# Windowed attention ahead of two feed-forward layers: the softmax division moved from the probabilities to the output

## The chip, the cores and the metric

One of the eight cores of a Trainium2 chip runs the whole program. Its engines are TensorE (PE for its matmuls, PEld for its weight loads), VectorE (DVE), ScalarE (ACT), GpSimd (POOL) and SyncE (SP, which here only issues DMAs). Each works through its own list of instructions in order and waits on semaphores for the others. The metric is device time in microseconds of one execution; lower is better.

## The reference

Sixteen heads (2 batches of 8) of 768 positions and 64 columns attend to four sink positions and to the last 128 positions. The result, 1536 tokens by 512, goes through two feed-forward layers of 512 by 2048 by 512, each with its own activation.

```python
scores = scale * np.matmul(q, k.transpose(0, 1, 3, 2))
keep = is_sink | in_window
scores = np.where(keep, scores, -1000000000.0)
a = np.exp(scores - np.max(scores, axis=-1, keepdims=True))
a = a / (np.sum(a, axis=-1, keepdims=True) + 1e-09)
x = np.matmul(a, v)                       # then (tokens, heads * head_dim)
h = x @ w_in                              # first layer
g = np.where(h >= 1, h, np.where(h <= -1, 0.0, (h + 1) ** 2 / 4))
x = g @ w_out
h = x @ w2_in                             # second layer
g = np.where(h > 0.0, h, np.exp(np.minimum(h, 0.0)) - 1.0)
out = g @ w2_out
```

## The kernel before

**Attention.** The queries are cut into six segments (three for each batch) of two blocks of 128 rows, and the heads into four pairs, which gives 24 jobs (a segment and a pair). A job runs in five steps. `st_T` turns q and k by PE transposes (L444) and copies them to SBUF (L446); POOL writes the four sink keys behind each block of keys (L458, L463). `st_S`, once for each of the two query blocks, multiplies (L488) and has DVE apply the mask and take the maximum (L492, tile `nb`) and ACT the exponential with its row sum (L494, tile `sm`). With the second block come the reciprocals `r` of the sums (L501, L502), the four sink columns of both blocks, normalised, into `psn` (L505), and the normalisation of all of P: on DVE by head (L514), or on POOL for both heads at once (L509) for the jobs 8 to 15 (`POOLED`). `st_X` turns P by transposes (L536) and copies it (ACT, L538). `st_V` multiplies it by v (L561), and DVE copies the pair's output, with features on partitions and queries along the columns, to `xb` (L564).

After the fourth pair of a segment `st_sink` adds what the sink positions give: it turns `psn` for all heads (L573), splits the result into a rounded part and a remainder (`pst`, L575 to L577), multiplies it by the sinks' values `vs` (L585), adds that to `xb` (L588), and splits the sum into `xh` and `xl` (ACT L590, POOL L591), the input of the feed-forward layers. All of the layers' products are made of such pairs, three products for one.

**Feed-forward layers.** An item is a block of 512 tokens (three) and 128 of the 2048 hidden columns (16), for each of the two layers: 96 items. An item has 12 products for `h` (L172), the activation `g` and its split into `gh` and `gl` (L179 to L189), and 12 products into four sums `y` (L211), which follow two items later. Its weights are split anew into `wh` (ACT, L160) and `wl` (POOL, L161). The weights come from memory as 64-bit numbers, in units of 128 columns or rows: ACT, then DVE turn a unit into float32 (L140, L141 and L144, L145, L147), 32 units for each layer, the first layer's within its first 13 items.

**What sets the order.** The first two segments (jobs 0 to 7) run ahead of the first item. From then on every item calls `between` four times, and each call runs one step of the attention, until the six segments are done. From this program a scheduler makes the lists of the five engines, merging steps by its own estimate of their times; the lists are then fixed. Pools set how far work can run ahead: four P tiles, two PSUM banks for the attention once the items have begun (`bank`), one `xb`.

**The store.** In the last items the output sums are copied to one of two tiles of the pool `mt` (L274) and written out.

## Time and profile before

| what | value |
|---|---|
| median of 3 runs | 692.01 us (691.42 to 694.39) |
| the profiled execution, its own time | 691.88 us |
| its span, first to last instruction | 689.7 us |
| busy in the span: PE, DVE, ACT, POOL | 660.4, 406.0, 459.9, 315.3 us |
| mean granted clock of TensorE | 0.983 of 2.4 GHz |
| PE in h and y (L172, L211), instructions | 1152 and 1128 of 3112 |

The busy time of an engine is the union of its instructions' durations in the trace. Matmuls overlap in the pipeline, so that PE is shown as busy also where it starts instructions at less than its rate; what it starts, and what it waits for, is read from the order of time and from the list of waits. An idle time is put down to the engine whose semaphore came last before the instruction began. "issue" is time in which an engine waited for nothing that the profile shows. Shares of the whole span average over stages with different limits, so the rows below are by stage.

### The profile page before, as it was taken

To read this page: it belongs to the slowest core of one execution; us is meant where nothing else is said; L and a number is where in the kernel's file an instruction comes from. 1 tells how busy PE (TensorE), PEld (TensorE's weight loads), DVE (VectorE), ACT (ScalarE), POOL (GpSimd) and SP (SyncE) were. 2 spreads that over 40 slices of the span, in tenths; PEclk is the share of its full clock that TensorE was granted. 3 is DMA by queue.
4 is the path that set the end of the run, shared out by engine and by line. 5 is a ranking of instruction groups with operands and counts; after the bars stand their busy time and mean duration, and the time that the engine had idled before them with its cause. 6 is when DMAs were issued, how large, how long until landed. Compare 5 with 4: busy or idle time off the path is not lost.

```text
span 689.7 us, 9414 instructions
## 1 busy us (share of the span) xinstructions
PE 660.4 (96%) x3112; PEld 506.3 (73%) x3112; DVE 406.0 (59%) x839; ACT 459.9 (67%) x944; POOL 315.3 (46%) x278
## 2 busy tenths in 40 slices
PE   5998987889999999999999999999999999999996
PEld 3566665666767777788878888888888888888884
DVE  5788999899665565322788878777532222322221
ACT  5799887787766766555768877777655555555552
POOL 2324464474523433444445655555544444444431
PEclk9699999899999999999999999999999999999999
DMA  6465564366121000000143323232010000100001
GB/s 168 104 179 155 160 183 139 114 207 180 32 54 39 12 13 13 0 1 1 61 153 95 119 92 92 93 100 83 0 62 2 0 1 0 60 3 0 1 0 67
DMA packets 71018, 48.96 MB, mean 71 GB/s; under 512 B 48944, under 2 KB 65328, under 8 KB 70960
## 3 DMA queue, kind: packets, MB, share of 16 engines
q1 hardware_dynamic: 70672, 48.27, 24.2%
q8 instruction: 26, 0.43, 0.3%
q14 instruction: 32, 0.26, 0.1%
q10 hardware_dynamic: 288, 0.00, 0.0%
HBM read 45.11 MB, written 3.15 MB: 70 GB/s over the span
## 4 chain that ended last, share of the span: by engine, by line
PE 77%; DVE 14%; issue 4%; ACT 3%; SPq 1%; POOL 1%; DMA 0%; POOLq 0%; DVEq 0%; ACTq 0%
PE h L172 33%; PE y L211 32%; PE S L488 4%; DVE ca L145 3%; DVE F L147 3%; PE ops L561 3%; PE tps L536 3%; DVE ca L144 2%; DVE P L492 1%; DVE g L181 1%; DVE gl L189 1%; SPq L387 1%; PE kps L444 1%; ACT P L494 1%; PE qps L444 1%
## 5 line engine op out<-in xcount | busy, mean ns | idle before, releaser
L161 POOL TENSOR_TENSOR wl<-F,wh 128x512 fp32r<-128x512 f32 x192 | 262.8, 1372 | 296.4 <-ACT wh L160 261.4
L160 ACT CAST wh<-F 128x512 fp32r<-128x512 f32 x192 | 117.6, 617 | 99.1 <-PE h L172 88.8
L172 PE MATMUL h<-xh,wh 128*128 128x512 f32 x384 | 155.2, 405 | 2.4 <-DVE g L181 2.4
L172 PE MATMUL h<-xl,wh 128*128 128x512 f32 x384 | 152.0, 396 | 0.5 <-POOL xl L591 0.5
L172 PE MATMUL h<-xh,wl 128*128 128x512 f32 x384 | 151.7, 395 | 0.0
L188 ACT CAST gh<-g 128x512 fp32r<-128x512 f32 x96 | 59.6, 621 | 66.0 <-DVE g L185 36.1
L189 DVE TENSOR_TENSOR gl<-g,gh 128x512 fp32r<-128x512 f32 x96 | 73.0, 761 | 51.2 <-ACT gh L188 50.8
L185 DVE SCALAR_TENSOR_TENSOR g<-g,h 128x512 f32<-128x512 f32 x48 | 33.0, 687 | 115.5 <-ACT g L184 115.4
L172 PEld LDWEIGHTS h<-xh,wh 128*128 128x128 f32 x384 | 71.9, 187 | 22.4 <-DVE g L181 3.2
L147 DVE CUSTOM_DVE_ANT_0 F<-ca,F 128x1024 uint16<-128x1024 uint16 x64 | 81.6, 1275 | 5.7 <-DVE ca L145 1.8
L172 PEld LDWEIGHTS h<-xh,wl 128*128 128x128 f32 x384 | 71.9, 187 | 17.7
L172 PEld LDWEIGHTS h<-xl,wh 128*128 128x128 f32 x384 | 72.0, 188 | 16.5 <-POOL xl L591 1.1
L211 PE MATMUL y<-gh,wh 128*128 128x512 f32 x192 | 79.7, 415 | 0.0
L211 PE MATMUL y<-gl,wh 128*128 128x512 f32 x192 | 76.4, 398 | 0.0
L211 PE MATMUL y<-gh,wl 128*128 128x512 f32 x192 | 75.9, 395 | 0.0
L211 PE MATMUL y<-wl,gh 128*128 128x512 f32 x184 | 72.2, 392 | 0.0
L211 PE MATMUL y<-wh,gh 128*128 128x512 f32 x184 | 71.8, 390 | 0.0
L211 PE MATMUL y<-wh,gl 128*128 128x512 f32 x184 | 71.6, 389 | 0.0
L494 ACT ACTIVATE P<-P,nb 128x260 f32<-128x260 f32 (+1 forms) x96 | 46.7, 488 | 19.3 <-DVE nb L492 18.7
L181 DVE SCALAR_TENSOR_TENSOR g<-h,g 128x512 f32<-128x512 f32 x48 | 32.9, 685 | 44.2 <-ACT g L180 44.2
L145 DVE SCALAR_TENSOR_TENSOR ca<-st,ca 128x512 int32<-128x512 int32 x64 | 52.9, 826 | 1.5
L140 ACT ACTIVATE ca<-st 128x512 f32<-128x512 f32 x64 | 43.0, 672 | 5.2 <-DVE F L147 4.3
(103 smaller groups left out, 920.0 us busy)
## 6 DMA issues: line engine op xcount, KB each, us to landing
st<-in_moe_w_in_dram SPq DMA_DIRECT2D x32, 512.0 KB, 3.9
st<-in_moe_w_out_dram SPq DMA_DIRECT2D x32, 512.0 KB, 3.6
qn<-in_q_dram SPq DMA_DIRECT2D x48, 64.0 KB, 2.1
kn<-in_k_dram SPq DMA_DIRECT2D x32, 96.0 KB, 2.3
vn<-in_v_dram SPq DMA_DIRECT2D x32, 96.0 KB, 2.2
out_dram<-o SPq DMA_DIRECT2D x12, 256.0 KB, 2.2
kn<-in_k_dram SPq DMA_DIRECT2D x16, 64.0 KB, 2.9
vn<-in_v_dram SPq DMA_DIRECT2D x16, 64.0 KB, 2.1
```

The source lines that it names most:

```text
L140: nc.scalar.activation(a, w1.bitcast(F32), AF.Copy, scale=2.0 ** -112)
L145: nc.vector.scalar_tensor_tensor(out=ai, in0=w1, scalar=-0x80000000, in1=ai, op0=ALU.bitwise_and, op1=ALU.bitwise_or)
L147: nc.vector.tensor_tensor(out=r, in0=ai, in1=r, op=ALU.add)
L160: nc.scalar.copy(hi, src)
L161: nc.gpsimd.tensor_tensor(out=lo, in0=src, in1=f32(hi), op=ALU.subtract)
L172: nc.tensor.matmul(h, lhsT=w[:, k * 128:(k + 1) * 128], rhs=x[:, k, c0:c0 + n], start=(k == 0 and p == 0), stop=(k == self.KD - 1 and p == 2))
L181: nc.vector.scalar_tensor_tensor(out=g, in0=h, scalar=1.0, in1=g, op0=ALU.max, op1=ALU.min)
L185: nc.vector.scalar_tensor_tensor(out=g, in0=g, scalar=-1.0, in1=h, op0=ALU.add, op1=ALU.max)
L188: ac = nc.scalar.copy(gh, g)
L189: dv = nc.vector.tensor_tensor(out=gl, in0=g, in1=f32(gh), op=ALU.subtract)
L211: nc.tensor.matmul(self.y[c], lhsT=a, rhs=b, start=(first and p == 0), stop=(last and p == 2))
L494: ac = nc.scalar.activation(o, o, AF.Exp, bias=nb[:, n, h:h + 1], scale=-1.0, accum_out=sm[:, n, h:h + 1])
```

## The change

P stays as the exponential leaves it. `st_S` loses L501 to L514; in place of L505 POOL copies the four sink columns of each head, one instruction of eight columns for each job and block (48 in all), to one tile `psn` of a segment, and the row sums of all eight heads of a segment go to one tile `sm`. `st_sink` begins with four DVE instructions on 16 columns: the sums get 1e-9, the reciprocals, their rounded part and the remainder of the rounding, the last two behind the sinks in `psn`. The transposes then turn 48 columns instead of 32, ACT makes one more copy (16 partitions), and `pst` has 112 rows instead of 96. A constant `one` of 112 by 512, built once by POOL, has ones in the rows of the reciprocals: its product with `pst` (L595 in the new numbering) gives each reciprocal in all 64 rows of its head, `rps`, in a second PSUM bank beside `xps`. DVE adds `xps` to `xb` as before and then multiplies by `rps`. `vs` gets 16 rows of zeros. The store uses the tiles `g` and `ca` in place of `g` and `o`, which frees SBUF. Line numbers of the new kernel differ by -1 up to `vsink` and by +8 to +13 behind it.

```diff
--- before.py
+++ after.py
@@ -17,7 +17,6 @@
 LAG = 2
 EXACT = 16
 FIRST = 9
-POOLED = range(8, 16)
 NSINK = 4
 BLK = 128
 KW = BLK + NSINK
@@ -271,7 +270,8 @@
     def store(self, c, r0):
 
         nc = self.nc
-        o = self.t_p.tile([128, self.DM], F32, tag="go"[c // 2 % 2], name="o")
+        pool, tag = ((self.t_p, "g"), (self.c_p, "ca"))[c // 2 % 2]
+        o = pool.tile([128, self.DM], F32, tag=tag, name="o")
         if c % 2:
             nc.scalar.copy(o, self.y[c])
         else:
@@ -356,7 +356,16 @@
             return self.vs[b]
         nc, const, H, D = self.nc, self.const, self.H, self.D
         R = H * NSINK
+        L = 3 * R + 2 * H
         if self.sel is None:
+
+            self.one = const.tile([L, H, D], F32R, tag="one", name="one")
+            one = const.tile([L, H], F32, tag="oneh", name="oneh")
+            nc.gpsimd.memset(one, 0.0)
+            for j in range(2):
+                nc.gpsimd.affine_select(out=one[3 * R:], in_=one[3 * R:], pattern=[[-1, H]],
+                                        compare_op=ALU.not_equal, fill=1.0, base=-j * H, channel_multiplier=1)
+            nc.gpsimd.tensor_copy(self.one, one.unsqueeze(2).to_broadcast([L, H, D]))
             self.sel = const.tile([3 * R, H], F32, tag="sel", name="sel")
             nc.gpsimd.memset(self.sel, 1.0)
             for g in range(3):
@@ -371,8 +380,9 @@
         nc.scalar.copy(part[R:2 * R], raw)
         nc.vector.tensor_tensor(out=part[2 * R:], in0=raw, in1=f32(part[0:R]), op=ALU.subtract)
         shape = [3 * R, H, D]
-        self.vs[b] = const.tile(shape, F32R, tag="vs", name="vs")
-        nc.gpsimd.tensor_tensor(out=self.vs[b], in0=f32(part).to_broadcast(shape),
+        self.vs[b] = const.tile([L, H, D], F32R, tag="vs", name="vs")
+        nc.gpsimd.memset(f32(self.vs[b][3 * R:]), 0.0)
+        nc.gpsimd.tensor_tensor(out=self.vs[b][0:3 * R], in0=f32(part).to_broadcast(shape),
                                 in1=self.sel.unsqueeze(2).to_broadcast(shape), op=ALU.mult)
         return self.vs[b]
 
@@ -473,9 +483,12 @@
         if n == 0:
             P = []
             nb = self.s_p.tile([128, nq, 2], F32, tag="nb", name="nb")
-            sm = self.s_p.tile([128, nq, 2], F32, tag="sm", name="sm")
-            st["P", pr] = P, nb, sm
-        P, nb, sm = st["P", pr]
+            st["P", pr] = P, nb
+            if "sm" not in st:
+                st["sm"] = self.s_p.tile([128, nq, self.H], F32, tag="sm", name="sm")
+                st["ps"] = self.s_p.tile([128, nq, self.H * (NSINK + 2)], F32, tag="psn", name="psn")
+        P, nb = st["P", pr]
+        sm = st["sm"]
         P.append(self.p_p.tile([128, 2, WP], F32, tag="P", name="P"))
         qb = q0 + n
         ty = min(qb, 2)
@@ -491,27 +504,12 @@
             o = P[n][:, h, 0:W]
             dv = nc.vector.tensor_tensor_reduce(out=o, in0=S[h], in1=self.mask[ty], op0=ALU.add, op1=ALU.min,
                                                 scale=-self.scale, scalar=3.0e38, accum_out=nb[:, n, h:h + 1])
-            ac = nc.scalar.activation(o, o, AF.Exp, bias=nb[:, n, h:h + 1], scale=-1.0, accum_out=sm[:, n, h:h + 1])
-        if n == nq - 1:
-            if self.first is None:
-                self.first = (ac.ins, dv.ins)
-            if "ps" not in st:
-                st["ps"] = [self.s_p.tile([128, self.H, NSINK], F32, tag=f"psn{i}", name=f"psn{i}") for i in range(nq)]
-            r = self.s_p.tile([128, nq, 2], F32, tag="r", name="r")
-            nc.vector.tensor_scalar(out=r, in0=sm, scalar1=1.0e-9, scalar2=None, op0=ALU.add)
-            nc.vector.reciprocal(out=r, in_=r)
-            for i in range(nq):
-                W = KW if q0 + i == 0 else WP
-                nc.vector.tensor_tensor(out=st["ps"][i][:, 2 * pr:2 * pr + 2, :], in0=P[i][:, :, BLK:KW],
-                                        in1=r[:, i, :].unsqueeze(2).to_broadcast([128, 2, NSINK]), op=ALU.mult)
-                if self.jobs.index((seg, pr)) in POOLED:
-                    o = P[i][:, :, 0:W]
-                    nc.gpsimd.tensor_tensor(out=o, in0=o, in1=r[:, i, :].unsqueeze(2).to_broadcast([128, 2, W]),
-                                            op=ALU.mult)
-                    continue
-                for h in range(2):
-                    o = P[i][:, h, 0:W]
-                    nc.vector.tensor_scalar(out=o, in0=o, scalar1=r[:, i, h:h + 1], scalar2=None, op0=ALU.mult)
+            ac = nc.scalar.activation(o, o, AF.Exp, bias=nb[:, n, h:h + 1], scale=-1.0,
+                                      accum_out=sm[:, n, 2 * pr + h:2 * pr + h + 1])
+        sinks = st["ps"][:, n, 2 * pr * NSINK:2 * (pr + 1) * NSINK]
+        nc.gpsimd.tensor_copy(sinks.rearrange("p (h s) -> p h s", h=2), P[n][:, :, BLK:KW])
+        if n == nq - 1 and self.first is None:
+            self.first = (ac.ins, dv.ins)
 
     def chunks(self, q0):
 
@@ -566,26 +564,39 @@
     def st_sink(self, seg, st):
         nc, D, nq = self.nc, self.D, self.nq
         b, q0, t, c0 = seg
-        R = self.H * NSINK
+        H = self.H
+        R = H * NSINK
         N = nq * 128
-        bank = self.bank([R, N], "sps")
+
+        ps, sm = st["ps"], st["sm"]
+        nc.vector.tensor_scalar(out=sm, in0=sm, scalar1=1.0e-9, scalar2=None, op0=ALU.add)
+        nc.vector.reciprocal(out=sm, in_=sm)
+        nc.vector.tensor_copy(ps[:, :, R:R + H].bitcast(F32R), sm)
+        nc.vector.tensor_tensor(out=ps[:, :, R + H:], in0=sm, in1=ps[:, :, R:R + H], op=ALU.subtract)
+        bank = self.bank([R + 2 * H, N], "sps")
         for n in range(nq):
-            nc.tensor.transpose(bank[:, n * 128:(n + 1) * 128], st["ps"][n].rearrange("p h s -> p (h s)"), self.idn)
-        pst = self.xb_p.tile([3 * R, N], F32R, tag="pst", name="pst")
-        nc.scalar.copy(pst[0:R], bank)
-        nc.scalar.copy(pst[2 * R:], bank)
-        nc.vector.tensor_tensor(out=pst[R:2 * R], in0=bank, in1=f32(pst[0:R]), op=ALU.subtract)
+            nc.tensor.transpose(bank[:, n * 128:(n + 1) * 128], ps[:, n, :], self.idn)
+        pst = self.xb_p.tile([3 * R + 2 * H, N], F32R, tag="pst", name="pst")
+        nc.scalar.copy(pst[0:R], bank[0:R])
+        nc.scalar.copy(pst[2 * R:3 * R], bank[0:R])
+        nc.scalar.copy(pst[3 * R:], bank[R:])
+        nc.vector.tensor_tensor(out=pst[R:2 * R], in0=bank[0:R], in1=f32(pst[0:R]), op=ALU.subtract)
         xh, xl = self.xts[t]
         vs = self.vsink(b)
         yield
         for p2 in range(0, self.H // 2, 2):
-            bank = self.bank([128, 2, N], "xps")
+            bank, rep = [self.bank([128, 2, N], nm) for nm in ("xps", "rps")]
             for j in range(2):
-                pr = p2 + j
-                nc.tensor.matmul(bank[:, j, :], lhsT=vs[:, 2 * pr:2 * pr + 2, :].rearrange("p h d -> p (h d)"), rhs=pst,
+                h = 2 * (p2 + j)
+                nc.tensor.matmul(bank[:, j, :], lhsT=vs[:, h:h + 2, :].rearrange("p h d -> p (h d)"), rhs=pst,
+                                 start=True, stop=True)
+            for j in range(2):
+                h = 2 * (p2 + j)
+                nc.tensor.matmul(rep[:, j, :], lhsT=self.one[:, h:h + 2, :].rearrange("p h d -> p (h d)"), rhs=pst,
                                  start=True, stop=True)
             x = st["xb"][:, p2:p2 + 2, :]
             nc.vector.tensor_tensor(out=x, in0=bank, in1=x, op=ALU.add)
+            nc.vector.tensor_tensor(out=x, in0=x, in1=rep, op=ALU.mult)
             hi = xh[:, p2:p2 + 2, c0:c0 + N]
             nc.scalar.copy(hi, x)
             nc.gpsimd.tensor_tensor(out=xl[:, p2:p2 + 2, c0:c0 + N], in0=x, in1=f32(hi), op=ALU.subtract)
```

The rows that follow are from the engines' lists. DVE, third segment (the first that ends among the items), from the last g ahead of its end: the reciprocals and sink columns (r, psn), the weights' units (ca, F), the sinks (pst, xb). Before:

```order
L144 TENSOR_SCALAR ca<-ca 128x512
L145 SCALAR_TENSOR_TENSOR ca<-st,ca 128x512
L501 TENSOR_SCALAR r<-sm 128x4
L502 RECIPROCAL r<-r 128x4
L564 COPY xb<-ops 128x256
L505 TENSOR_TENSOR psn_1496<-P,r 128x8
L505 TENSOR_TENSOR psn_1497<-P,r 128x8
L147 ISA F<-ca,F 128x1024
L144 TENSOR_SCALAR ca<-ca 128x512
L145 SCALAR_TENSOR_TENSOR ca<-st,ca 128x512
L144 TENSOR_SCALAR ca<-ca 128x512
L577 TENSOR_TENSOR pst<-sps,pst 32x256
```

After, from the end of the segment's scores to the remainder:

```order
L180 SCALAR_TENSOR_TENSOR g<-h,g 128x512
L572 TENSOR_SCALAR sm<-sm 128x16
L562 COPY xb<-ops 128x256
L146 ISA F<-ca,F 128x1024
L188 TENSOR_TENSOR gl<-g,gh 128x512
L573 RECIPROCAL sm<-sm 128x16
L143 TENSOR_SCALAR ca<-ca 128x512
L574 CAST psn<-sm 128x2x8
L144 SCALAR_TENSOR_TENSOR ca<-st,ca 128x512
L575 TENSOR_TENSOR psn<-sm,psn 128x2x8
L146 ISA F<-ca,F 128x1024
L505 ISA P,nb<-S,mask_150 128x132
```

and, 14 rows further on, up to the first sum:

```order
L146 ISA F<-ca,F 128x1024
L562 COPY xb<-ops 128x256
L143 TENSOR_SCALAR ca<-ca 128x512
L144 SCALAR_TENSOR_TENSOR ca<-st,ca 128x512
L143 TENSOR_SCALAR ca<-ca 128x512
L146 ISA F<-ca,F 128x1024
L144 SCALAR_TENSOR_TENSOR ca<-st,ca 128x512
L583 TENSOR_TENSOR pst<-sps,pst 32x256
L146 ISA F<-ca,F 128x1024
L598 TENSOR_TENSOR xb<-xps,xb 128x512
```

The reciprocals moved behind the whole segment, and between them and `pst` stand parts of four units (F four times) and other work, where parts of two stood.

PE at the same place, between the matmuls of an item. Before:

```order
L211 MATMUL y_1136<-gh,wh_1422 128x512
L585 MATMUL xps<-pst,vs 128x256 x2
L211 MATMUL y_1136<-gl,wh_1422 128x512
L211 MATMUL y_1136<-gh,wl_1423 128x512
L211 MATMUL y_1137<-gh,wh_1422 128x512
L211 MATMUL y_1137<-gl,wh_1422 128x512
L211 MATMUL y_1137<-gh,wl_1423 128x512
```

After:

```order
L210 MATMUL y_1097<-gh,wl_1372 128x512
L591 MATMUL xps<-pst,vs 128x256 x2
L595 MATMUL rps<-pst,one 128x256 x2
L210 MATMUL y_1098<-gh,wh_1371 128x512
L210 MATMUL y_1098<-gl,wh_1371 128x512
L210 MATMUL y_1098<-gh,wl_1372 128x512
L210 MATMUL y_1099<-gh,wh_1371 128x512
L591 MATMUL xps<-pst,vs 128x256 x2
L210 MATMUL y_1099<-gl,wh_1371 128x512
```

The first pair of sink products moved two matmuls back, and two products with `one` (rps) stand behind it; the second pair's are further on.

POOL, jobs 9 to 11, between the weights' splits wl. Before:

```order
L509 TENSOR_TENSOR P<-P,r 128x520 x2
L161 TENSOR_TENSOR wl_1301<-F,wh_1300 128x512
L458 COPY sk_1266<-kh 128x4
L463 COPY kh<-sk_1266 128x2x4
L161 TENSOR_TENSOR wl_1305<-F,wh_1304 128x512
L161 TENSOR_TENSOR wl_1419<-F,wh_1418 128x512
L509 TENSOR_TENSOR P<-P,r 128x520 x2
L161 TENSOR_TENSOR wl_1423<-F,wh_1422 128x512
```

After:

```order
L510 COPY psn<-P 128x8
L160 TENSOR_TENSOR wl_1151<-F,wh_1150 128x512
L510 COPY psn<-P 128x8
L160 TENSOR_TENSOR wl_1256<-F,wh_1255 128x512
L468 COPY sk_1221<-kh 128x4
L473 COPY kh<-sk_1221 128x2x4
L160 TENSOR_TENSOR wl_1260<-F,wh_1259 128x512
L510 COPY psn<-P 128x8
```

Each multiplication of P, one for a block, gave way to a copy of eight columns at about the same place.

## Rows read from the trace of the kernel before

**Rows 1.** Stages: length, busy PE, PEld, DVE, ACT, POOL, clock, DMA share, GB/s.

```profile
0.00:62.00 62.00, 52.71 (x287) 31.76 (x287) 45.92 (x200) 48.31 (x141) 17.44 (x41) 0.89 0.61 152
62.00:162.00 100.00, 87.40 (x435) 61.84 (x436) 93.95 (x183) 81.22 (x185) 54.86 (x49) 0.97 0.53 159
162.00:290.00 128.00, 126.79 (x692) 94.33 (x690) 76.23 (x208) 85.14 (x193) 50.72 (x49) 1.00 0.16 38
```

**Rows 2.** The chain that ended last from 62 to 162 us, shares by line.

```profile
by line: DVE F L147 16.4%; DVE ca L145 15.9%; issue 9.7%; DVE ca L144 9.0%; PE y L211 6.4%; DVE P L492 5.4%; PE h L172 5.3%; PE S L488 4.8%; DVE gl L189 4.3%; DVE g L181 4.2%; PE tps L536 4.1%; DVE psn L505 1.9%; DVE r L501 1.6%; DVE xb L56
```

**Rows 3.** DVE by line, 62 to 162 us: busy, mean ns, idle time before.

```profile
L147 DVE CUSTOM_DVE_ANT_0 F<-ca,F 128x1024 uint16<-128x1024 uint16 x24 | 26.7, 1113 | 1.3
L145 DVE SCALAR_TENSOR_TENSOR ca<-st,ca 128x512 int32<-128x512 int32 x25 | 23.9, 955 | 0.4
L144 DVE TENSOR_SCALAR ca<-ca 128x512 int32<-128x512 int32 x25 | 15.6, 625 | 0.3 <-ACT ca L140 0.3
...
L505 DVE TENSOR_TENSOR psn<-P,r 128x8 f32<-128x8 f32 x12 | 2.4, 241 | 0.0
...
L501 DVE TENSOR_SCALAR r<-sm 128x4 f32<-128x4 f32 x6 | 2.1, 343 | 0.0
L588 DVE TENSOR_TENSOR xb<-xps,xb 128x512 f32<-128x512 f32 x2 | 1.4, 676 | 0.0
L502 DVE RECIPROCAL r<-r 128x4 f32<-128x4 f32 x6 | 1.0, 174 | 0.1
```

**Rows 4.** POOL: L509 from 62 to 162 us; L463 (min/median/max ns) over the span.

```profile
L509 POOL TENSOR_TENSOR P<-P,r 128x520 f32<-128x520 f32 (+1 forms) x12 | 15.8, 1333 | 9.6 <-DVE psn L505 9.5
...
L463 POOL COPY kh<-sk x16: 189/250/738, 6.8 to 142.9; 128x8 f32<-128x8 f32 x8, 128x12 f32<-128x12 f32 x8
```

**Rows 5.** Timeline of DVE and POOL at four places: start us, us, instruction.

```profile
68.18 0.69 DVE L147 CUSTOM_DVE_ANT_0 F<-ca,F 128x1024 uint16<-128x1024 uint16 x1
...
69.25 0.69 DVE L145 SCALAR_TENSOR_TENSOR ca<-st,ca 128x512 int32<-128x512 int32 x1
...
75.41 2.97 POOL L509 TENSOR_TENSOR P<-P,r 128x520 f32<-128x520 f32 x2 [1.31 <-DVE psn L505]
76.15 1.32 DVE L147 CUSTOM_DVE_ANT_0 F<-ca,F 128x1024 uint16<-128x1024 uint16 x1
...
151.12 1.84 POOL L509 TENSOR_TENSOR P<-P,r 128x264 f32<-128x264 f32 x2
...
152.08 1.43 DVE L145 SCALAR_TENSOR_TENSOR ca<-st,ca 128x512 int32<-128x512 int32 x1
```

**Rows 6.** DVE, L514 from 0 to 62 us.

```profile
L514 DVE TENSOR_SCALAR P<-P,r 128x260 f32<-128x260 f32 (+1 forms) x32 | 10.3, 383 | 0.0
```

**Rows 7.** The start: ACT and PE in order of time, then two stretches by engine.

```profile
10.54 0.24 ACT L370 CAST vpart<-vraw 32x64 fp32r<-32x64 f32 x1 [1.85 <-DMA vraw<-in_v_dram]
...
11.96 0.50 ACT L494 ACTIVATE P<-P,nb 128x260 f32<-128x260 f32 x1
...
14.76 1.58 PE L536 MATMUL tps<-idn,P 128*128 128x128 f32 x6 [5.21 <-DVE P L514]
...
9.50:14.30 4.80, 0.05 (x1) 0.00 (x0) 2.42 (x14) 3.72 (x17) 0.72 (x1) 1.00 0.92 266
14.30:28.00 13.70, 12.49 (x49) 8.06 (x50) 9.08 (x35) 9.93 (x29) 3.42 (x7) 0.50 0.48 104
```

**Rows 8.** PE in order of time at the first segment's sinks.

```profile
40.68 0.74 PE L585 MATMUL xps<-pst,vs 96*128 96x256 f32 x4
41.26 1.04 PE L536 MATMUL tps<-idn,P 128*128 128x128 f32 x8
```

**Rows 9.** PE's waits from 62 to 162 us: total us, times, longest.

```profile
PE tps L536 <- DVE nb L492: 3.2, 2, 1.8
...
PE xps L585 <- DVE pst L577: 2.2, 1, 2.2
PE h L172 <- DVE g L181: 2.2, 1, 2.2
```

## The prediction

> **What bounds the kernel now.** I first cut the span into stages and read for each which engine has no room left [rows 1]. From 0 to 62 us eight of the 24 attention jobs run, and TensorE (PE) is covered for 52.7 of 62 us. From 62 to 162 the first twelve feed-forward items run between seven further jobs, while the first layer's weights are converted on VectorE (DVE): DVE is busy 93.95 of 100 us, PE 87.4. From 162 to 290 the other jobs run between items, and PE is busy 126.79 of 128. After 290 the attention is through and only matrix work is left. So time can be given back before 162 us and not later, and whatever is added to PE after 162 is paid in full.
>
> Then the chain that ended last, cut at the middle stage [rows 2]: its largest shares are the three conversion instructions on DVE (16.4, 15.9 and 9.0%); the normalisation's small instructions stand on it as well (L505 1.9, L501 1.6). Last, the same stage by line on DVE [rows 3], POOL's normalising multiplications [rows 4], and both engines in order of time [rows 5]: DVE there is not only full, its conversions are stretched.
>
> **The change part by part.** The sum is made against the profiled execution, 691.88 us, of which 689.7 are the span; it lies 0.13 below the median of the three runs, 692.01. What lies around the span I leave as it is.
>
> *0 to 62 us.* 32 multiplications L514 go from DVE, 10.3 us [rows 6], and with them 18 L505 and nine pairs L501 and L502; four products with the replicated reciprocals come. DVE is busy only 45.9 of 62 us there [rows 1], so this work is worth what waits on it. First, the start: PE's first transposes begin at 14.76, released by L514 after 5.21 us of waiting; the last exponential that they read starts at 11.96 and lasts 0.50 [rows 7]. Without the normalisation they could start at 12.46, 2.3 earlier. What follows them hangs on the third job's loads and on ACT's list as before, so I take 1.4 (bounds 0 and 2.3). Second, PE gets eight more 256-column products, two times four. Four of the same shape (xps) started at 40.68 and the next instruction at 41.26 [rows 8]: 0.145 each, +1.2, on an engine that has no idle time here. Third, the end of the second segment: two products of 128x512 stand between the sums and the split, at L588's 0.68 each (its row is that of the next stage [rows 3]), +1.4; ACT makes a third copy of the transposed sinks, about 0.4 (an estimate, below the 0.50 of an exponential); the last job's four L514 are no longer ahead of its transposes, -1.3 (four times 10.3/32). Sum +0.3; bounds -0.6 and +1.7, by those of the start. The constant of ones is written by POOL between the first two copies of sink keys, one instruction of 512 columns; I cost it at nothing, since ACT, which the first scores go to, stands for its load until 10.54 anyway [rows 7]; without that cover it would cost about 1 us at the start.
>
> *62 to 162 us.* Removed from DVE: L505 2.4, L501 2.1, L502 1.0 [rows 3], together 5.5. The eight jobs from the ninth on had their multiplication on POOL, so no L514 goes here. Added: two chains of four instructions of 16 elements, each near the 174 ns of L502 (1.4), and two products at 0.676 (1.4). Net -2.7. Then the port. A conversion L147 takes 0.69 us and L145 0.69 when POOL is idle; beside a POOL multiplication L509 the first took 1.32 (at 76.15, POOL from 75.41) and the second 1.43 (at 152.08, POOL from 151.12) [rows 5]: the DVE instruction ends when POOL's does, plus its own time. Nine DVE instructions ran so beside an L509, that at 76.15 the first and that at 152.08 the last, and by their shares of the overlap were 5.0 us longer than usual. L509 goes entirely (12 here, 15.8 us of POOL [rows 4]), so -5.0. In its place come some 14 copies of eight elements; the nearest POOL copy (L463) takes 0.19 at least and 0.25 in the median [rows 4]. If none meets a conversion they cost nothing, if each does, 14 x 0.19 = 2.7; I take half, +1.4 (of L509's 15.8 us a third, 5.0, showed up on DVE). Sum -6.3, bounds -7.7 (free copies) and -3.1 (the second rival).
>
> The Trainium skill (SBUF — State Buffer, section "SBUF: two separate sides") says that VectorE and GpSimd share one port pair as an exclusive lock, and that the loser waits for the whole instruction of the other. By that rule it speaks against the sink copies, which are 48 new holders of the lock: at the full 2.7 us this stage would give -5.0 and the whole 688.9.
>
> Is DVE's gain on the path? PE waits in this stage, mostly for late DVE work: transposes 3.2 us, xps 2.2, h 2.2 [rows 9], 7.6 in these three. So PE has room to follow 6.3 us of DVE, and not much more.
>
> *162 to 290 us.* DVE, ACT and POOL are covered by PE, so their removals bring nothing. PE gets 12 products x 0.145 = +1.7 (bounds 1.7 and 8.3, the third rival). *After 290 us* the order has the same matrix work; the store's buffers move to a tile of the converter, idle by then: 0.
>
> Sum: 0.3 - 6.3 + 1.7 = -4.3, so 691.88 - 4.3 = **687.6 us**.
>
> **The rivals.** *First, the clock in the first stage.* PE was granted 2.4 GHz up to 14.3 us and 1.2 GHz from there to 28.0 [rows 7]; it had stood since 9.55, almost 5 us, before the clock fell. In that stretch PE is covered for 12.49 of 13.70 us and ACT busy 9.93. With transposes from 12.5 us on, the clock may stay up. Half of 12.49 can't be had, since ACT's 9.93 stay: at most 13.7 - 9.9 = 3.8, say 3.4. That gives 684.2. Against it: PE would still stand for 3 us, and between the transposes and the third job's loads.
>
> *Second, the middle stage gives half.* PE is covered for 87.4 of its 100 us already [rows 1] and gets four products more; the new order on DVE has one or two weight units more ahead of most g instructions (18 instead of 17 ahead of the sixth, 31 instead of 29 ahead of the eleventh, 32 ahead of the twelfth in both), so the late items may wait for PE where they waited for DVE. Half of 6.3 lost is 3.15: 690.8, no change that can be told.
>
> *Third, slower: PE stands at the sinks.* The reciprocals now come once a segment, in a chain at its end, with POOL's last sink copy ahead of the transposes, and PE, which works in order, stands at xps until DVE has made pst. In the third segment three or four conversion instructions stood between the last L505 and L577, and PE waited 2.2 us at xps [rows 9]. Now four whole units stand there: 4 x (0.625 + 0.955 + 1.113) = 10.8 us by the means of the stage [rows 3], against some 3.3 (L147, L145 and two L144): the wait could grow by up to 7.5 there. That decides only if DVE then finds nothing to do; it also falls on the last three segments, where PE is the bound, at 2.2 each once the chain ends later than PE's nine matmuls up to xps. 687.6 + 7.5 x 0.4 + 3 x 2.2 = 697.2. From some 8 us of such waits on the result is slower. Against it: PE waits for almost nothing at the sinks after 162 us, when it is busy 126.79 of 128 [rows 1].
>
> That the change doesn't do what it says can be left aside: the multiplications are out of the program.
>
> **How the numbers follow.** Within 0.5% (3.5 us, about what a measurement of this kernel can tell from no change) means 688.5 to 695.5. The forecast's own case, 685.5 to 690, gets 0.46: 0.30 of it faster, 0.16 the same. The first rival 0.14, faster. The second 0.28, the same. The third 0.12: 0.10 slower, 0.02 the same. So faster 0.44, the same 0.46, slower 0.10. For 8 in 10 the range leaves out the lower half of the first rival and most of the third: 683.5 to 694.
>
> **What would show it.** Right: from the first h matmul to the twelfth g on DVE some 6 us less; no conversion beside a POOL instruction of over a microsecond other than wl, xl and vs; first transposes near 12.5 us; the stretch behind the last sink longer by 1 to 2 us at most. Wrong: granted clock 1.00 between 14 and 28 us (first rival); DVE below 90% busy in the middle stage with the stage as long as before (second); PE waits for pst or for psn of over 2 us in several segments (third); conversions stretched by POOL copies as often as by L509.

## The result and the profile after

The changed kernel takes 684.74 us in the median of 13 executions, the kernel before 694.2 in 13 beside it on the same chip: a ratio of 0.9863, 95% interval 0.9839 to 0.9887, some 9.5 us less. The profiled execution of the changed kernel takes 683.62 us (span 681.8), 8.3 less than the one of before. The forecast was 687.6, the range 683.5 to 694: faster, as the forecast said, but by twice as much.

One thing has to be known to read the times. Executions of one kernel differ by how long TensorE is granted 1.2 instead of 2.4 GHz (twice the missing share of the mean clock, times the span): the kernel before took 690.2 us with 17.9 us of it and 697.2 with 37.5. So beside the medians I compare executions with about the same time at 1.2 GHz. Alike in that, at 19 to 24 us, the kernel before has 691.3 to 693.4 and the changed one 683.6 to 685.1: 7.5 us less. The other 2 of the 9.5 are the clock: 27.7 us at 1.2 GHz near the median of before, 21.8 near that of after.

The stages of the changed kernel, by the same view as [rows 1] (length, busy PE, PEld, DVE, ACT, POOL, clock, DMA share, GB/s):

```profile
0.00:62.00 62.00, 52.40 (x283) 30.76 (x283) 36.62 (x141) 47.90 (x142) 19.32 (x61) 0.89 0.61 154
62.00:162.00 100.00, 95.95 (x487) 67.58 (x488) 89.00 (x188) 88.11 (x203) 47.12 (x55) 0.98 0.61 179
162.00:290.00 128.00, 127.84 (x701) 96.35 (x700) 58.08 (x140) 84.20 (x188) 55.02 (x65) 1.00 0.10 22
```

In the middle stage PE and DVE have changed places: PE from 87.4 to 95.95 of 100 us, DVE from 93.95 to 89.0. The chain that ended last, cut at the same stage as [rows 2], says it too: the conversions fell from 16.4, 15.9 and 9.0% to 3.6, 3.8 and 2.3%, and PE leads.

```profile
by line: PE h L171 28.4%; PE y L210 17.6%; PE S L501 8.7%; PE ops L559 5.5%; issue 5.1%; PE tps L534 4.6%; DVE ca L144 3.8%; DVE F L146 3.6%; DVE ca L143 2.3%; ACT ca L139 1.8%; ACT pt L536 1.8%; DVE g L180 1.7%; ACT P L507 1.7%; POOL xl L6
```

The conversions by line, 62 to 162 us, as in [rows 3] (L147, L145 and L144 are now L146, L144 and L143):

```profile
L146 DVE CUSTOM_DVE_ANT_0 F<-ca,F 128x1024 uint16<-128x1024 uint16 x27 | 23.0, 853 | 2.3 <-ACT F L140 1.5
L144 DVE SCALAR_TENSOR_TENSOR ca<-st,ca 128x512 int32<-128x512 int32 x27 | 20.6, 765 | 0.3
L143 DVE TENSOR_SCALAR ca<-ca 128x512 int32<-128x512 int32 x27 | 16.6, 617 | 0.1
```

Two or three more units fit into the stage, at 0.85 and 0.77 us for the two long instructions instead of 1.11 and 0.96.

Where the 7.8 us between the two profiles' last h matmuls come from, by three marks: the first h matmul starts at 60.6 before and 62.8 after (+2.2), from there to the end of the twelfth g it is 110.1 and 100.4 (-9.7, some 1.2 of it the clock: 6.83 and 3.41 us of that stretch are at 1.2 GHz, 0.36 us of time for one), and from the first h of the thirteenth item to that of the twenty-seventh 116.0 and 115.8. From there to the last h both take 385.4. The forecast had +0.3, -6.3 and +1.7.

The start, PE in order of time. One transpose of P runs alone at 10.11, the others start at 12.20 (before: 14.76, [rows 7]). But then PE waits for ACT's copies, and the next scores (L501), which wait for POOL, come only 1.03 us earlier than L488 of before.

```profile
12.20 0.93 PE L534 MATMUL tps<-idn,P 128*128 128x128 f32 x5 [1.79 <-ACT P L507]
15.19 0.69 PE L534 MATMUL tps<-idn,P 128*128 128x128 f32 x2 [2.06 <-ACT pt L536]
...
17.81 0.80 PE L501 MATMUL S<-kh,qh 64*128 64x132 f32 x2 [0.86 <-POOL kh L473]
```

The same place in the kernel before:

```profile
18.84 0.78 PE L488 MATMUL S<-kh,qh 64*128 64x132 f32 x2 [0.61 <-POOL kh L463]
```

The end of the first stage in the changed kernel, PE in order of time:

```profile
60.89 0.55 PE L454 MATMUL kps<-idn,kn 128*128 128x128 f32 x3 [1.04 <-DVE xb L598]
...
64.39 0.80 PE L171 MATMUL h<-xl,wh 128*128 128x512 f32 x1 [0.90 <-POOL xl L602]
```

The same microseconds on DVE and POOL:

```profile
59.56 1.28 DVE L598 TENSOR_TENSOR xb<-xps,xb 128x512 f32<-128x512 f32 x2
60.76 1.27 DVE L599 TENSOR_TENSOR xb<-xb,rps 128x512 f32<-128x512 f32 x2
...
62.88 3.15 POOL L602 TENSOR_TENSOR xl<-xb,xh 128x512 fp32r<-128x512 f32 x2
```

Sum and product of the output take 2.5 us on DVE (before: the sum alone, 1.29 us). The next transposes (L454) wait 1.04 us for the sum, and the first product that needs xl waits 0.90 us for POOL. POOL's xl needs the product and ACT's copy xh, which starts at 61.97; it also stands behind a wl in POOL's list (61.65 to 62.92), which before came after xl.

### The profile page after: what moved, and what is told of

It is laid out like the page before. It is cut to its first block, busy times and chain, and to the rows that moved or that the text cites. A ratio compares the mean times of both kernels' runs of the same rounds, so it can differ in the third digit from the quotient of the medians.

```text
span 681.8 us, 9397 instructions
## 1 busy us (share of the span) xinstructions
PE 661.8 (97%) x3136; PEld 506.7 (74%) x3136; DVE 371.9 (55%) x715; ACT 462.0 (68%) x950; POOL 308.6 (45%) x316
## 4 chain that ended last, share of the span: by engine, by line
PE 86%; DVE 6%; ACT 4%; issue 3%; POOL 1%; POOLq 0%; DVEq 0%; ACTq 0%
PE h L171 37%; PE y L210 35%; PE S L501 5%; PE ops L559 3%; PE tps L534 3%; DVE ca L144 1%; PE kps L454 1%; DVE F L146 1%; ACT P L507 1%; DVE ca L143 1%; PE qps L454 1%; PE y L267 1%; PE warmup L738 1%; POOL wl L160 0%; DVE g L180 0%
## 5 line engine op out<-in xcount | busy, mean ns | idle before, releaser
L188 DVE TENSOR_TENSOR gl<-g,gh 128x512 fp32r<-128x512 f32 x96 | 70.9, 739 | 50.2 <-ACT gh L187 49.8
L146 DVE CUSTOM_DVE_ANT_0 F<-ca,F 128x1024 uint16<-128x1024 uint16 x64 | 75.3, 1177 | 6.7 <-DVE ca L144 1.8
L144 DVE SCALAR_TENSOR_TENSOR ca<-st,ca 128x512 int32<-128x512 int32 x64 | 48.2, 754 | 1.4
L505 DVE CUSTOM_DVE_ANT_0 P<-S,mask 128x260 f32<-128x260 f32 (+1 forms) x96 | 35.4, 402 | 22.2 <-PE S L501 18.6
```

Source lines behind the costliest of these rows:

```text
L144: nc.vector.scalar_tensor_tensor(out=ai, in0=w1, scalar=-0x80000000, in1=ai, op0=ALU.bitwise_and, op1=ALU.bitwise_or)
L146: nc.vector.tensor_tensor(out=r, in0=ai, in1=r, op=ALU.add)
L188: dv = nc.vector.tensor_tensor(out=gl, in0=g, in1=f32(gh), op=ALU.subtract)
L505: dv = nc.vector.tensor_tensor_reduce(out=o, in0=S[h], in1=self.mask[ty], op0=ALU.add, op1=ALU.min, scale=-self.scale, scalar=3.0e38, accu ...
```

## The experiments

Twelve kernels ran, in four groups, each group on one chip beside the kernel before. "At 1.2 GHz" is worked out as above; the last column has the executions with 16.5 to 25 us of it.

| kernel | median, us | ratio to before (95%) | executions, us (us at 1.2 GHz) |
|---|---|---|---|
| before, all groups | 694.2 to 695.3 | | 690.0 to 690.2 (16.5 to 17.9), 691.3 to 691.8 (19.3), 691.7, 693.4 (23.4, 23.5), 693.9 (24.9) |
| changed, first result | 684.7 | 0.9863 (0.9839 to 0.9887) | nine, 683.6 to 685.1 (20.5 to 23.2) |
| a_again | 687.5 | 0.987 (0.982 to 0.9919) | 684.1 (20.5), 684.3, 685.0 (21.8, 21.9) |
| b_no509 | 688.8 | 0.989 (0.9853 to 0.9926) | 686.1 (23.3), 685.6 (24.6) |
| a_port | 695.7 | 0.9994 (0.9963 to 1.0026) | six, 692.2 to 694.2 (22.1 to 23.5) |
| a_inplace | 691.8 | 0.9961 (0.9929 to 0.9993) | ten, 690.7 to 693.6 (22.1 to 24.9) |
| b_no514 | 696.5 | 1.0002 (0.9941 to 1.0064) | 692.5 (22.1) |
| b_none | 686.0 | 0.9878 (0.9823 to 0.9933) | 683.2, 683.6 (19.1) |
| a_nodiv | 682.1 | 0.982 (0.9768 to 0.9872) | 679.2, 679.3 (19.0) |
| a_cpact | 690.1 | 0.9944 (0.9897 to 0.9991) | 688.1, 688.8 (22.0), 690.0 (24.8) |
| a_copies4 | 685.6 | 0.9886 (0.9839 to 0.9934) | 684.9 (17.8), 685.7 (20.5), 685.5, 685.6 (23.2) |
| a_cpdve | 688.8 | 0.9887 (0.9838 to 0.9937) | 683.2, 683.4 (17.7) |
| a_fill | 687.7 | 0.9909 (0.9879 to 0.994) | seven, 686.1 to 689.2 (17.8 to 24.8) |
| a_xldve | 689.7 | 0.9864 (0.98 to 0.9928) | 683.0 (21.8), 682.8 (23.2) |

My theory was that POOL's multiplications held up DVE's conversions on a common port. The rivals: it is the number of DVE instructions; or the transposes had waited for the multiplications.

**The changed kernel again** (a_again), for the three kernels of its group.

> The changed kernel itself, beside the next three on one chip, so that these can be compared with it: 0.986 of the kernel before, as in its first result.

It came out as the first time, 684.1 to 685.0 at like clock.

**The kernel before without L509** (b_no509).

```
                 if self.jobs.index((seg, pr)) in POOLED:
-                    o = P[i][:, :, 0:W]
-                    nc.gpsimd.tensor_tensor(out=o, in0=o, in1=r[:, i, :].unsqueeze(2).to_broadcast([128, 2, W]),
-                                            op=ALU.mult)
                     continue
```

> The kernel before without POOL's multiplication of P (L509) in the jobs 8 to 15; their probabilities stay unnormalised and nothing divides later, so this part of the computation is left out. The lists of PE, DVE, ACT and SP are the same, instruction for instruction. My theory (the shared port: nine DVE instructions were 5.0 us longer beside L509): 5 us less in the middle stage, 0.993 of the kernel before; conversions stretched by wl as before (15 us of the stage). Rival one, the gain came from fewer instructions on DVE: nothing here, 1.000. Rival two, the multiplication stood between the exponentials and the transposes of P: also some microseconds less here, but with it the copy into a spare tile in the next run costs nothing.

686.1 and 685.6 us at 23.3 and 24.6 us at 1.2 GHz, against 691.7, 693.4 and 693.9 of before at 23.4 to 24.9: 6.7 us less by the first two of these, 7.2 by all three. Against a straight line through the 62 executions of before in the four groups (0.36 us for each at 1.2 GHz) all six executions lie 4.8 to 7.8 us lower, 6.3 in the mean. The lists of all other engines are the same, so fewer DVE instructions can't be the reason. DVE's long conversion from the first h to the twelfth g, in the kernel before:

```profile
L147 DVE CUSTOM_DVE_ANT_0 F<-ca,F 128x1024 uint16<-128x1024 uint16 x27 | 29.3, 1087 | 1.4
```

The same line in the kernel without L509:

```profile
L147 DVE CUSTOM_DVE_ANT_0 F<-ca,F 128x1024 uint16<-128x1024 uint16 x27 | 26.5, 982 | 1.4
```

The surprise is in the parts. What an instruction takes beyond its usual time (0.69 us for L147 and L145, 0.42 for L144, 0.68 for L189) I divide among the POOL instructions beside it by their shares of the overlap; differences of under 1 us between such figures say nothing. So worked out, L509 had stretched the conversions (L144, L145, L147, L189) by 5.2 us, and that went; but wl's part went from 15.1 to 11.5 as well. POOL's instructions had stood one behind the other: before, nine unbroken runs of POOL of over 2 us made up 39.9 us of that stretch, without L509 six runs 21.7. In this profile 13.7 us of the stretch are at 1.2 GHz, so that DVE also waits more for PE there; wl's share is a hint here, and the next two runs show it with equal lists.

**The port alone** (a_port): the changed kernel, with the multiplications back on POOL, into a tile that nobody reads.

```
...
+        if n == nq - 1 and self.jobs.index((seg, pr)) in range(8, 16):
+            for i in range(nq):
+                W = KW if q0 + i == 0 else WP
+                nc.gpsimd.tensor_tensor(out=self.scr[:, :, 0:W], in0=P[i][:, :, 0:W],
+                                        in1=nb[:, i, :].unsqueeze(2).to_broadcast([128, 2, W]), op=ALU.mult)
```

> The changed kernel, with POOL multiplying both P tiles of the jobs 8 to 15 into a spare tile that nobody reads: 16 instructions of the size of L509, at the place in POOL's list that they had, on nobody's path; all other lists unchanged. Port theory: the conversions are stretched again, 5 us more than the changed kernel, 0.993 of the kernel before. Rival (only the waiting for the multiplication cost time): no change against the changed kernel, 0.986. Rival (PE is the bound of the middle stage now, at 95.95 of 100 us busy): less than 2 us.

692.9 us in the median of six against 684.6 of the changed kernel at nearly like clock: 8.3 us more (some 0.6 of it for 23.5 instead of 21.8 us at 1.2 GHz), as much as the whole change had gained, for 16 instructions on which nobody waits. The stretch from the first h to the twelfth g in the changed kernel (columns as in the table of the stages):

```profile
62.80:163.10 100.30, 96.38 (x493) 67.94 (x493) 88.87 (x188) 88.41 (x203) 46.32 (x55) 0.98 0.61 177
```

The same stretch in a_port:

```profile
73.80:181.90 108.10, 99.85 (x486) 69.69 (x486) 97.68 (x187) 88.24 (x202) 60.22 (x68) 0.96 0.59 164
```

DVE has the same list and is busy 97.68 instead of 88.87 us. This profile is of an execution of 703.9 us, and some of the length is clock: 8.7 us of the stretch are at 1.2 GHz against 3.4. The row of the next run is freer of that. What happens to one conversion, POOL and DVE in a_port in order of time:

```profile
93.95 1.50 POOL L517 TENSOR_TENSOR scr<-P,nb 128x520 f32<-128x520 f32 x1
95.41 1.28 POOL L160 TENSOR_TENSOR wl<-F,wh 128x512 fp32r<-128x512 f32 x1
95.81 1.43 DVE L146 CUSTOM_DVE_ANT_0 F<-ca,F 128x1024 uint16<-128x1024 uint16 x1 [1.28 <-ACT F L140]
```

The multiplication is followed at once by wl, which it had kept waiting, and the conversion that comes next (0.69 us when POOL is idle) ends 0.5 us after wl: 1.43 us. The stretch by the multiplications themselves is 3.7 us, that by wl 13.1 instead of 6.3. Since the order of all other lists is that of the changed kernel, it is shown that the multiplications cost this time without anyone waiting for them; that they do so partly by themselves and partly by moving wl onto the conversions is worked out from the overlaps.

**The port and the wait** (a_inplace): the same 16 multiplications in place, by ones, ahead of the transposes.

```
...
+        if n == nq - 1 and self.jobs.index((seg, pr)) in range(8, 16):
+            for i in range(nq):
+                W = KW if q0 + i == 0 else WP
+                o = P[i][:, :, 0:W]
+                nc.gpsimd.tensor_tensor(out=o, in0=o, in1=self.un.unsqueeze(2).to_broadcast([128, 2, W]),
+                                        op=ALU.mult)
```

> The changed kernel, with the same 16 multiplications on POOL, but in place and by ones, so that the transposes of P wait for them as they waited for L509; all other lists unchanged. Port theory: like the run with the spare tile, 0.993 of the kernel before, at most 1 us more. Theory of the wait: 5 us or more above the run with the spare tile.

691.6 us in the median of ten, 7.0 above the changed kernel (some 0.5 of it clock) and not above a_port. The stretch from the first h to the twelfth g, in an execution of 692.1 us with 6.8 us of the stretch at 1.2 GHz:

```profile
62.80:171.30 108.50, 99.18 (x493) 68.73 (x493) 98.38 (x188) 88.73 (x203) 61.10 (x69) 0.97 0.58 164
```

It is 8.2 us longer than in the changed kernel (1.2 of it by the 3.4 us more at 1.2 GHz), and DVE is busy 9.5 us longer with the same list. That the transposes wait for the multiplication costs nothing that can be seen; that rival falls.

**The kernel before without L514** (b_no514).

```
-                for h in range(2):
-                    o = P[i][:, h, 0:W]
-                    nc.vector.tensor_scalar(out=o, in0=o, scalar1=r[:, i, h:h + 1], scalar2=None, op0=ALU.mult)
```

> The kernel before without DVE's multiplications of P (L514) in the jobs 0 to 7 and 16 to 23; those probabilities stay unnormalised, so this part of the computation is left out. 64 instructions of 0.38 us, some 20 us of DVE's time, go; POOL's L509 stay. My theory: only the start (-1.4 us) and the last job ahead of the first item (-1.3) are worth something, the middle stage and the stage bound by PE nothing: 2.7 us less, 0.996 of the kernel before. Rival, DVE's busy time counts: a third of the 20 us or more, 0.990 or lower.

At like clock 692.5 against some 692; at 15.1 us of 1.2 GHz 689.0 against 690.0 to 690.9 (13.8 to 16.5), at 31.8 us 694.0 against 696.3 and 697.1 (31.9, 32.0): between nothing and 2.7 us less, some 1.4 in the mean. Twenty us of DVE's time are worth hardly anything, so the rival falls. The scheduler orders this kernel a little anew (PE's list differs in 33 places, with the same instructions), so the 1.4 us hold the new order too. And where it is worth something was not only where I had said; see the next run.

**The kernel before without any multiplication of P** (b_none): both edits together.

```
-                if self.jobs.index((seg, pr)) in POOLED:
-                    o = P[i][:, :, 0:W]
-                    nc.gpsimd.tensor_tensor(out=o, in0=o, in1=r[:, i, :].unsqueeze(2).to_broadcast([128, 2, W]),
-                                            op=ALU.mult)
-                    continue
-                for h in range(2):
-                    o = P[i][:, h, 0:W]
-                    nc.vector.tensor_scalar(out=o, in0=o, scalar1=r[:, i, h:h + 1], scalar2=None, op0=ALU.mult)
```

> The kernel before without any multiplication of P (neither L509 nor L514); the sums, the reciprocals and the sinks stay, the normalisation of P is left out, and nothing is added. What both removals are worth together, free of what the change adds: 6.5 (the run without L509) and 2.7, so some 9 us less, 0.987 of the kernel before, about the time of the changed kernel. If the changed kernel gains by its shorter DVE chain too (2.7 us by my sum), this kernel stays behind it by that.

683.2 and 683.6 at 19.1 us of 1.2 GHz, against 691.3 to 691.8 of before at 19.3: 8.1 less, which is 6.7 and 1.4. PE, DVE and ACT have the same lists here as in b_no514, so the two runs price L509 a second time, in another order: 689.0 and 681.3 us at 15 us of 1.2 GHz, 694.0 and 688.6 at 32 to 33, 5 to 8 us. The stretch from the thirteenth to the twenty-seventh item, where the forecast had said that removals bring nothing, in the kernel before:

```profile
173.30:289.30 116.00, 115.23 (x631) 85.96 (x629) 64.95 (x182) 75.04 (x170) 44.28 (x43) 1.00 0.11 24
```

In b_no509:

```profile
175.30:291.30 116.00, 115.22 (x630) 86.11 (x629) 64.89 (x182) 75.13 (x170) 44.24 (x43) 1.00 0.11 24
```

In b_none:

```profile
166.70:280.70 114.00, 114.00 (x630) 85.66 (x629) 51.85 (x146) 74.60 (x168) 44.14 (x43) 1.00 0.11 25
```

In the changed kernel:

```profile
165.70:281.50 115.80, 115.64 (x644) 87.12 (x641) 52.37 (x131) 76.71 (x173) 47.09 (x58) 1.00 0.11 24
```

In a_nodiv, the next run:

```profile
161.70:275.90 114.20, 114.04 (x630) 85.50 (x629) 48.90 (x126) 75.94 (x171) 47.31 (x57) 1.00 0.11 25
```

The length of the stretch is the first number behind the two times. With L514 gone it is 2.0 shorter (114.0, also in b_no514), at full clock throughout; the products with ones bring it back to 115.8 (a_nodiv against the changed kernel, where PE's lists for this stretch are otherwise the same). PE's waits there in the kernel before, none of which b_none has:

```profile
PE xps L585 <- DVE pst L577: 0.5, 1, 0.5
PE qps L444 <- DVE xb L564: 0.3, 1, 0.3
```

Laid side by side, PE's two lists part in steps: 0.4 us at that qps (the copy of xb that it waits for stands behind four L514, one of them 1.38 us long beside a wl), 0.5 at that xps, 0.2 at two smaller places, and 0.8 where the scores of two heads, apart in the list of before, stand together in the new one. So 1.2 us are waits for DVE work behind L514 and 0.8 are PE's own order. The transposes of P take 6.25 us in both.

**The changed kernel without the division** (a_nodiv).

```
-                nc.tensor.matmul(rep[:, j, :], lhsT=self.one[:, h:h + 2, :].rearrange("p h d -> p (h d)"), rhs=pst,
-                                 start=True, stop=True)
...
-            nc.vector.tensor_tensor(out=x, in0=x, in1=rep, op=ALU.mult)
```

> The changed kernel without the products with ones (rps) and without the multiplication of the output by them (L599): the division is left out, sums, reciprocals and their transposes stay. It prices what the change adds behind the sinks. By my sum 2.9 us of PE (20 products beyond the first segment's, 0.145 each, after the start), 1.4 of DVE at the end of stage one and 1.4 in the middle stage: 5 us less than the changed kernel, 0.980 of the kernel before. Rival, these instructions lie beside other work (stage three was no longer than before although it has twelve more products): within 1.5 us of the changed kernel, 0.985.

679.2 and 679.3 us at 19.0 of 1.2 GHz; the changed kernel has 683.6 to 684.7 at 20.5. With 0.5 off for that (before grew by 7.0 us from 17.9 to 37.5 us at 1.2 GHz, 0.36 for one, on 1.5 us), 4.3 is the price of the division (684.1 - 0.5 - 679.3); by the profiles 2.4 at the end of the first stage (first h at 60.4 instead of 62.8), 1.3 in the middle (99.1 instead of 100.4) and 1.6 in the stretch above, 5.3 together, with 3.4 us less at 1.2 GHz in the middle. My sum had 5 (its parts add up to 5.7) and the rival at most 1.5: the work is on the path. The lists are ordered anew in the first two stages (18 places on PE besides the products left out), and the 1.3 of the middle are about what its clock gives. Against b_none, which has neither multiplication nor division but the old chain by job, a_nodiv is 4.1 us faster at the same clock: that is what one chain a segment, with the sink columns copied by POOL, saves against two L505 and one L501 and L502 a job, together with the order of the lists, which differs between the two (37 places on PE, 52 on DVE). How much is the chain's own was not separated.

**The sink copies on ACT** (a_cpact).

```
-        nc.gpsimd.tensor_copy(sinks.rearrange("p (h s) -> p h s", h=2), P[n][:, :, BLK:KW])
+        nc.scalar.copy(sinks.rearrange("p (h s) -> p h s", h=2), P[n][:, :, BLK:KW])
```

> The changed kernel with the 48 copies of the unnormalised sink columns on ACT instead of POOL. My sum has 1.4 us for 14 such copies on the shared port in the middle stage, the full price by the rule of the lock is 2.7; the trace of the changed kernel puts 0.7 us on them. If that is their price, this run is 0.7 to 1.4 us faster than the changed kernel or, with ACT's some 15 instructions more in a stage where it is busy for 88 of 100 us, the same or slower: 0.985 to 0.990 of the kernel before.

688.1 and 688.8 at 22.0: 4 us slower than the changed kernel. The scheduler orders much anew here (58 places in DVE's list alone), and wl stretches the conversions by 15.1 us instead of 6.3 although POOL has less to do. So the run does not price the copies; the next two do. Nor does the stretch alone make the time: in a_nodiv wl stretches the conversions by some 10.7 us, and its middle is the shortest of all, 99.1 us. A stretch costs where something that PE needs comes late by it.

**Three more copies behind each sink copy** (a_copies4).

```
...
+        for _ in range(3):
+            nc.gpsimd.tensor_copy(self.scr, P[n][:, :, BLK:KW])
```

> The changed kernel with each of the 48 sink copies on POOL followed by three more of the same shape into a spare tile: 144 more short POOL instructions, 45 of them in the middle stage; all other lists unchanged. If each such copy holds DVE up for its own 0.19 us, 8.5 us more in the middle stage; at half of that, as my sum took it, 4.3; at the share that the trace of the changed kernel shows (0.7 us for 15 copies) 2.1. So 0.989 to 0.999 of the kernel before; under 0.989 the copies are free.

684.9 to 685.7 us, 0.9 above the changed kernel for 144 copies: the 48 that the change adds cost about 0.3. The extra copies in the stretch from the first h to the twelfth g:

```profile
L513 POOL COPY scr<-P 128x8 f32<-128x8 f32 x45 | 14.5, 322 | 1.8
```

They take 0.32 us in the mean and not their 0.19 (0.35 in the 37 places beside a DVE instruction, 0.19 in the 8 others), and by the shares of the overlap they stretch no conversion: it is the copies that wait. The stretch by wl is some 1.5 us above that in the changed kernel.

**The sink copies on DVE** (a_cpdve).

```
-        nc.gpsimd.tensor_copy(sinks.rearrange("p (h s) -> p h s", h=2), P[n][:, :, BLK:KW])
+        nc.vector.tensor_copy(sinks.rearrange("p (h s) -> p h s", h=2), P[n][:, :, BLK:KW])
```

> The changed kernel with the 48 sink copies on DVE, the consumer side of the port, instead of POOL; ACT's list is unchanged, PE's but for four places. DVE gets 15 more instructions of 0.17 to 0.24 us in the middle stage (2.6 to 3.6 us), less the 0.7 of stretch that goes: if DVE still sets the length of that stage, 2 to 3 us more than the changed kernel, 0.990; if PE does (95.95 of 100 us busy), within 1 us of it, 0.986.

683.2 and 683.4 at 17.7 us of 1.2 GHz, and 688.5 to 689.2 at 28.8 and 28.9, where the changed kernel has 689.5 and 689.6: the same. DVE's 15 additional copies in the middle are 3.5 us of work, and the stretch is 100.7 us long against 100.4. DVE has room, so it no longer sets this stage; that PE does now is read from its 95.95 of 100 us.

**PE kept at work at the start** (a_fill).

```
+                if h == 0 and i == 1 and self.jobs[0] == (seg, pr):
+                    for _ in range(8):
+                        nc.tensor.matmul(bank[:, 2, :], lhsT=self.idn, rhs=self.idn, start=True, stop=True)
                 nc.tensor.transpose(bank[:, i, :], P[n][:, h, o:o + 128], self.idn)
```

> The changed kernel with eight needless products of the identity with itself on PE, where it stood from 10.4 to 12.2 us, into a bank that the next transposes overwrite. A test of my first rival (the clock of the first stage fell because PE stood): if that is so, the stretch of 13.65 us at 1.2 GHz from 13 us on shrinks or goes, and up to 3.4 us with it: 0.981 of the kernel before. If the fall has another cause (PE also stood from 13.1 to 15.2), 1.2 GHz is granted as before and the time stays within 1 us of the changed kernel.

Stretches of a_fill at the start:

```profile
9.64:13.05 3.41, 2.69 (x21) 2.34 (x22) 1.28 (x9) 2.13 (x9) 0.29 (x2) 1.00 0.87 253
13.05:16.47 3.42, 1.02 (x8) 0.78 (x9) 1.12 (x2) 3.42 (x13) 1.41 (x4) 1.00 0.97 223
16.47:26.71 10.24, 9.41 (x39) 5.55 (x38) 5.61 (x19) 6.97 (x22) 2.07 (x7) 0.50 0.39 89
```

The clock falls 3.4 us later, and comes back at the same time, so that 10.24 us are left at 1.2 GHz instead of 13.65; it now falls after the next gap of PE. In the 13 other profiles the first fall lies between 11.85 and 14.32 us and lasts 13.65 us or more; here it comes at 16.47. The first h matmul starts at 61.5 instead of 62.8. But the kernel as a whole is slower, 686.1 to 689.2: the lists are ordered anew here too, wl stretches the conversions by 12.6 us, and the middle takes 103.8. This one run agrees with the mechanism of the first rival, but its gain was not had.

**xl on DVE** (a_xldve), the try at a better kernel.

```
-            nc.gpsimd.tensor_tensor(out=xl[:, p2:p2 + 2, c0:c0 + N], in0=x, in1=f32(hi), op=ALU.subtract)
+            nc.vector.tensor_tensor(out=xl[:, p2:p2 + 2, c0:c0 + N], in0=x, in1=f32(hi), op=ALU.subtract)
```

> The changed kernel with the remainder xl of the attention's output (L602, twelve instructions of 1.29 us on POOL in the median) made on DVE instead, some 0.68 us each like L188. If long POOL instructions on the shared port are what costs time, and DVE has room since the change (89 of 100 us busy in the middle stage, 11.2 us idle from the first h to the twelfth g), the 3.0 us by which xl stretched the conversions there go and 2.7 of DVE's work come, and the first product that waited 0.9 us for xl starts earlier: 0.5 to 2 us less than the changed kernel, 0.984 of the kernel before. If PE sets the middle stage now, no change, 0.986; if DVE still does, up to 2 us more.

682.8 and 683.0 us at 21.8 to 23.2 of 1.2 GHz, 1.6 less than the changed kernel; but only two executions of six lie there, the others have 40 us and more, and the median is 689.7. By the interval it can't be told from the changed kernel. Whether it is better stays open.

## Why the prediction was right in sign and too small

**What bounds the kernel.** Right: the middle stage was DVE's, and time could be given back there. The limit that I drew from three of PE's waits (7.6 us of room, [rows 9]) was too low: PE was idle for 12.6 of the 100 us [rows 1], and 9.7 us came out of the stage (8.5 without the clock). a_cpdve shows that DVE is no longer the bound.

**The port, -5.0.** The mechanism was right (b_no509, a_port, a_inplace), the size was off: 6.7 by removal, 7.0 and 8.3 by putting it back (6.5 and 7.7 without the clock). The step that failed counted the stretch by the overlap with L509 alone [rows 5]. It left out what L509 did to POOL's own queue: wl came late and in a row behind it, and stretched conversions that it would have missed. With the same lists wl stretches them by 6.3 us without and 12.4 to 13.1 with the multiplications. An instruction on the shared port has to be costed with what is queued behind it.

**The chains, -5.5 + 1.4, and the copies, +1.4.** Together -2.7 in the sum, -4.1 measured (a_nodiv against b_none), with the new order of the lists in it. The copies cost 0.3 and not 1.4 (a_copies4, equal lists). That the chains were sized well is not contradicted, but not shown either. The Trainium skill (SBUF — State Buffer, section "SBUF: two separate sides") has the pair of ports as a lock that goes to whoever starts first, for the whole instruction. I had read it as a price for DVE. The trace agrees with the lock, but the loser here is the copy: 0.32 us in the mean against 0.19 (a_copies4), and no conversion longer by it. The 688.9 that the rule's full price gave was too high.

**The first stage, +0.3, was +2.2.** What is added came out right: 3.0 us (1.2, 1.4 and 0.4) forecast, 2.4 by a_nodiv plus 0.6 for all else that tells it from b_none (first h at 60.4 there, 59.8 in b_none). What is removed failed: -2.7 forecast (start and last job), -0.8 measured (b_none 59.8, before 60.6; the lists differ in order). The first transposes did come at 12.20, but only 1.0 us of that reached the next scores, and by the end of the stage other waits had taken it.

**After 162 us, +1.7, was -0.2.** The products with ones cost 1.6, as worked out. The step that failed is "their removals bring nothing": without L514 the stretch is 2.0 us shorter (116.0 to 114.0). Two waits on DVE, for pst and for the bank that the copy of xb sets free, both behind L514, and two smaller delays make 1.2 of it; 0.8 are PE's own new order. The busy share of 115.23 in 116.0 hid most of it: only 0.77 us are shown as idle. The transposes of P, which read what L514 wrote, lost nothing.

The sum of the measured parts, at like clock: -6.7 (L509), -1.4 (L514), -4.1 (chains and copies), +4.3 (division) make -7.9, against -7.5 found. That they close is no proof of the parts: the steps lead from the kernel before over b_none and a_nodiv to the changed kernel, and only the 6.7 and the 1.4 were taken apart independently (8.1 together in b_none). My sum was -4.3: 1.7 of the difference lie in the port, 1.4 in the chains and copies. By stages the forecast missed by +1.9, -3.4 and -1.9 us, so that two of the misses partly cancelled: that the whole stayed in the range is in part luck.

**The rivals.** The first (clock up in the first stage) did not happen: 1.2 GHz from 13.05 to 26.70 us. The second (the middle gives half) did not; its mechanism, PE as the next bound, came after 9.7 us instead of 3. The third did not: in the third segment PE waited 0.2 us for pst, where it had waited 2.2 [rows 9].

**The clock elsewhere**, in no term of my sum. Before, PE was covered for 1.28 of 3.46 us and the clock then fell for 6.83; nothing like it is in the changed kernel, which between 26.7 us and the last matmuls has one fall, of 3.41 us, after the waits at the end of its first stage. The kernel before, columns as above:

```profile
123.50:126.96 3.46, 1.28 (x6) 0.70 (x4) 3.43 (x4) 1.12 (x4) 1.94 (x2) 1.00 0.55 141
126.96:133.80 6.84, 6.80 (x21) 5.40 (x22) 5.56 (x11) 5.21 (x13) 2.31 (x3) 0.50 0.47 154
```

The changed kernel:

```profile
60.80:64.25 3.45, 2.35 (x9) 1.10 (x9) 3.45 (x7) 3.23 (x9) 2.60 (x2) 1.00 0.62 201
64.25:67.66 3.41, 3.27 (x8) 2.60 (x9) 3.38 (x5) 1.20 (x2) 1.77 (x2) 0.50 0.43 130
```

That a PE which stands less keeps its clock in most executions, and that this is the 2 us by which the medians differ beyond like clock, fits these rows but was not tested.

## What to carry to other kernels

Cost a POOL instruction beside a busy DVE by its own length and by what it pushes together behind it on POOL; the check is to put it back into a tile that nobody reads. Work taken from another engine can still be worth something where a covered engine waits in a few places behind it (here DVE multiplications ahead of the copy of xb and of pst): ask for the stretch's length with and without it, not for the busy share, and see that the order of the lists is the same in both. Compare executions at like granted clock before a difference of one per cent is explained.
